# Two-stage packed attention and routed experts in one kernel: gate roots on VectorE, and new orders in the head, the first softmax and the last stores

## The chip, the cores and the metric

One core of a Trainium2 chip runs the whole kernel. The metric is the device time of one execution in microseconds (us), as the median of several runs; lower is better.

## The reference

```python
def sm_attn(qq, kk, vv):                       # per batch and head, head_dim 64
    s = scale * qq @ kk.T                      # scale = 1/8
    a = softmax(s)                             # row maximum taken off, sum + 1e-9
    return a @ vv
p_packed = sm_attn(p, k, v)                    # 32 packed rows of 576 keys
x = sm_attn(q, p_packed, p_packed)             # 576 queries on the 32 packed rows
# x: 8 batches of 576 tokens of 8 heads * 64 = 512 values
logits = unit(x) @ unit(expert_emb).T / tau    # 8 experts
e = argmax(logits); gate = softmax(logits)[e]
out = gate * (relu(x @ w1[e]) @ w2[e])         # 512 -> 1024 -> 512, all float32
```

With the inputs that are drawn, a batch's tokens nearly always go to one expert. The kernel guesses that expert for each batch and does the batch with it; tokens that went elsewhere would be done by a loop at the end.

## The kernel before

The order of the instructions is the order in which the Python code emits them; each engine runs its own instructions strictly in that order, and waits at the first whose operands are not ready. So an instruction that waits holds everything behind it on its engine.

Batch 0 is done by a function of its own, `begin`, and by `ffn(late=True)`. `begin` loads k, v and q of batch 0 whole, scores 32 packed queries against the keys, exponentiates (`key_exp`), turns the probabilities on TensorE (`p1_turn`), copies them out of PSUM (`p1_evac`), and multiplies by v (`pack_values`). Beside it runs the generator `embeddings`: it loads the expert embeddings, makes their norms by a Newton root on GpSimd (POOL), takes a reciprocal on VectorE (DVE, line 144), scales the embeddings on GpSimd (L147, `en_sb`), turns them on TensorE (L151) and copies them to `enT`. `itau` is 1/tau: tau comes by a DMA from ScalarE's (ACT's) queue, and line 1072 takes the reciprocal. `key_sum` makes the inverse sums `ri`. `guess` multiplies the summed packed rows by `enT` (L531), takes the maximum on VectorE and hands the expert's number to SyncE (SP) or GpSimd, whose queue then loads that expert's w1 and w2. After the guess, `begin` turns the queries q in four banks of four blocks and one of the two last blocks (L1093), copies them out by ScalarE and VectorE, and makes the query scores (L1153).

The second softmax of batch 0 (`att2(first=True)`) follows a table of steps, `ORDS`: U unpacks a half from PSUM (L576), B is the maximum, S takes it off, X is the exponential, T the sum and reciprocal (L596 to L598), N the multiplication, R the turn (L611), H the high part of the split into two float32r parts (L617), L the low part (L622). 0 and 1 are the two halves of the queries, a and b the two groups of heads. `ENG` says for S0, S1, N0, N1, L0, L1 and then for the four low parts of G (`split_g`, L267) whether GpSimd (p) or VectorE (v) does them.

`ffn` forms the hidden rows: `rows_w1` multiplies the packed rows by w1 in two parts (L838) and copies the products g32 to SBUF (L850, the second of each part on VectorE); `hidden` multiplies by the softmax (L870), first for the half 0 in float32, then for the half 1 from the split parts G and AT; ScalarE and VectorE write the two parts of hT (L874, L875). The 64 rows left over go by L905. Then come four blocks of 128 rows times w2 (L923, three passes over eight parts each, 24 matmuls for a block). Every block has a PSUM bank of 3 (`ps`, tag pf), and a bank comes free when `store` has multiplied it by the gate (L1223, ScalarE): the third block of L923 takes the bank of the 64 rows.

`route` multiplies AT by the packed rows (L674), five blocks in two banks (`pb`); VectorE reduces the logits (L683) and ScalarE the squares (L690), and only then is the bank free. `counts` (L716, L719) counts the tokens of each expert. `gates` makes the gate: a Newton root of the squares, the scaled logits (L737), an exponential on ScalarE (L741), its sum and a reciprocal (L744 to L749). The root is done by VectorE for batches 1 to 7 and by GpSimd for batch 0:

```python
for n, _ in enumerate(rsqrt(ss, y, "g", nc.gpsimd if x is bat[0] else nc.vector)):
```

While batch 0 goes through `ffn`, a table `PLAN` says for each step of it which other work is emitted: q is a step of `begin`, s of the softmax of batch 0, G a low part of G, a a step of the attention of batch 1, d a query flip of batch 1, w a part of w2, r a step of `route`, g a step of `gates`. From batch 1 on the loop at the end of the program hands the steps out by rule. The results leave by four DMAs of 32 rows for each block from SyncE's queue (L1236); the last block of the last batch is done and stored in two halves of 256 columns.

## Time and profile before

| what | value |
|---|---|
| median of 3 runs | 454.12 us (453.8 to 454.4) |
| the profiled execution | 454.63 us, its span in the trace 453.0 us |
| TensorE (PE) | busy 435.5 us, 96% |
| VectorE (DVE) | busy 295.8 us, 65% |
| ScalarE (ACT) | busy 204.2 us, 45% |
| GpSimd (POOL) | busy 152.2 us, 34% |

The page cuts the span into 40 slices of 11.3 us. TensorE is at 9 tenths or more in nearly all of them; the two slices from 68 to 91 us are the only ones before the last with a granted clock of 8 tenths rather than 9 or more. Times below are us from the span's start. Busy time of TensorE is modelled; a matmul that waits behind a running one can be counted as busy.

### The profile page before, as it was taken

Reading aid. Unit: us, or ns where it says so; the run is one execution under the profiler, and the core shown is the slowest. Engines: PE = TensorE matmul, PEld = TensorE weight load, DVE = VectorE, ACT = ScalarE, POOL = GpSimd, SP = SyncE. Lnnn points to the kernel's source line nnn. Section 1 sums busy time; section 2 is a strip of 40 time slices with the busy share of each in tenths; the row PEclk is TensorE's granted clock in tenths of the full one; section 3 lists DMA queues with packets and bytes.
Section 4 is the critical chain, followed back from the end, with each engine's and each line's share of the span. In section 5 each row is a group of like instructions: output and inputs, shape, how many; then the busy total and the mean of one; then the engine's idle time right before and its main releaser. Section 6 shows DMA issues by size and latency. Waiting matters only on the chain.

```text
span 453.0 us, 10735 instructions
## 1 busy us (share of the span) xinstructions
PE 435.5 (96%) x3908; PEld 343.3 (76%) x3909; DVE 295.8 (65%) x901; ACT 204.2 (45%) x479; POOL 152.2 (34%) x199
## 2 busy tenths in 40 slices
PE   8998995999999999999999999999999999999993
PEld 3758763869687987879687887879788886879783
DVE  5677638458994698648894688747895588635500
ACT  3557512375336551376335561376335651466210
POOL 2455682242703153042612244041621336033200
PEclk9999998899999999999999999999999999999997
DMA  8898597558698577866698576866597524710022
GB/s 235 300 264 235 153 267 252 149 134 226 182 342 231 148 200 256 262 164 178 171 372 225 155 200 221 280 181 177 157 376 211 140 52 167 264 26 23 14 49 52
DMA packets 39868, 87.12 MB, mean 192 GB/s; under 512 B 11768, under 2 KB 19192, under 8 KB 39808
## 3 DMA queue, kind: packets, MB, share of 16 engines
q1 hardware_dynamic: 31248, 56.52, 45.4%
q0 software_dynamic: 7840, 29.36, 18.0%
q8 instruction: 33, 0.54, 0.5%
q10 hardware_dynamic: 720, 0.48, 0.4%
q14 instruction: 27, 0.22, 0.2%
HBM read 76.89 MB, written 9.44 MB: 191 GB/s over the span
## 4 chain that ended last, share of the span: by engine, by line
PE 87%; DVE 4%; POOL 2%; ACT 2%; DMA 2%; issue 2%; SPq 0%; ACTq 0%; POOLq 0%; DVEq 0%
PE pf L923 38%; PE pf L870 23%; PE pf L905 6%; PE pt L674 6%; PE pt L252 3%; PE pt L803 3%; PE pt L373 2%; PE pt L356 2%; DMA emb_sb<-in_moe_expert_emb 1%; DMA nat<-in_k 0%; DVE mx L581 0%; PE pf L1093 0%; PE pf L838 0%; POOL w2r L768 0%; DVE st L576 0%
## 5 line engine op out<-in xcount | busy, mean ns | idle before, releaser
L923 PE MATMUL pf<-w2s,hT 128*128 128x512 f32 (+1 forms) x792 | 191.5, 394 | 5.4 <-ACT o L1223 5.4
L923 PEld LDWEIGHTS pf<-w2s,hT 128*128 128x128 f32 x792 | 144.2, 191 | 44.5 <-issue 8.9
L779 POOL TENSOR_TENSOR w2s<-w2r,w2s 128x512 fp32r<-128x512 f32 x64 | 82.4, 1289 | 220.6 <-ACT w2s L778 218.2
L870 PE MATMUL pf<-AT,G 128*128 128x288 f32 x720 | 105.7, 299 | 1.4 <-ACT T L1194 1.1
L870 PEld LDWEIGHTS pf<-AT,G 128*128 128x128 f32 x720 | 97.7, 188 | 7.0 <-issue 2.8
L875 DVE SCALAR_TENSOR_TENSOR hT<-pf,hT 128x224 fp32r<-128x224 f32 (+1 forms) x128 | 52.6, 415 | 32.7 <-ACT hT L874 32.6
L874 ACT ACTIVATE hT<-pf 128x224 fp32r<-128x224 f32 (+1 forms) x128 | 48.5, 384 | 48.5 <-PE pf L870 47.0
L690 ACT ACTIVATE at<-pt 128x512 f32<-128x512 f32 (+1 forms) x40 | 23.9, 597 | 38.9 <-DVE lg L683 38.0
L778 ACT CAST w2s<-w2r 128x512 fp32r<-128x512 f32 x64 | 39.2, 615 | 1.2 <-issue 1.2
L1223 ACT ACTIVATE o<-pf,gate 128x512 f32<-128x512 f32 (+1 forms) x41 | 25.9, 634 | 24.8 <-PE pf L923 17.8
L674 PEld LDWEIGHTS pt<-ppx,AT 128*128 128x128 f32 (+1 forms) x240 | 33.1, 177 | 4.6 <-ACT at L690 0.8
L674 PE MATMUL pt<-ppx,AT 128*128 128x264 f32 (+1 forms) x240 | 36.0, 286 | 0.3 <-ACT at L690 0.3
L905 PE MATMUL pf<-w2r,h 128*64 128x256 f32 x256 | 34.6, 391 | 0.0
L683 DVE TENSOR_REDUCE lg<-pt 128x8 f32<-128x16 f32 (+1 forms) x40 | 6.6, 164 | 35.4 <-PE pt L674 35.4
L817 DVE TENSOR_TENSOR G<-pt,G 128x512 fp32r<-128x512 f32 x28 | 18.8, 690 | 15.3 <-ACT G L816 15.3
L590 ACT ACTIVATE st<-st 128x576 f32<-128x576 f32 (+1 forms) x17 | 11.2, 660 | 36.3 <-DVE st L587 33.7
L905 PEld LDWEIGHTS pf<-w2r,h 128*64 128x64 f32 x256 | 15.5, 136 | 10.2 <-issue 4.7
L280 DVE STREAM_TRANSPOSE kt<-nat 128x576 f32<-128x576 f32 x28 | 21.4, 766 | 0.0
L741 ACT ACTIVATE lg<-lg 128x40 f32<-128x40 f32 x8 | 1.9, 236 | 42.7 <-DVE lg L737 42.7
L768 POOL DMA_DIRECT2D w2r<-in_moe_w x28 | 19.9, 714 | 0.4 <-issue 0.4
L617 ACT CAST AT<-at 128x576 fp32r<-128x576 f32 x16 | 10.8, 674 | 20.2 <-DVE at L611 20.2
L275 DVE STREAM_TRANSPOSE kt<-nat 128x576 f32<-128x576 f32 x28 | 19.2, 737 | 0.0
(186 smaller groups left out, 479.2 us busy)
## 6 DMA issues: line engine op xcount, KB each, us to landing
nat<-in_q SPq DMA_DIRECT2D x112, 140.0 KB, 3.1
w1t<-in_moe_w POOLq DMA_DIRECT2D x14, 1024.0 KB, 7.9
w2r<-in_moe_w POOLq DMA_DIRECT2D x28, 512.0 KB, 10.1
nat<-in_k SPq DMA_DIRECT2D x96, 140.0 KB, 3.2
vn<-in_v SPq DMA_DIRECT2D x46, 192.0 KB, 4.2
out<-o SPq DMA_DIRECT2D x124, 64.0 KB, 1.7
nat<-in_k SPq DMA_DIRECT2D x4, 576.0 KB, 5.2
w1t<-in_moe_w SPq DMA_DIRECT2D x4, 512.0 KB, 5.2
```

The lines of the kernel that those rows point to most:

```text
L280: nc.vector.transpose(kt.rearrange("p (c i) -> p c i", i=32), t)
L674: nc.tensor.matmul(pt[:r, 512 * g : 512 * g + XW], AT[:, a, g, c * P : c * P + r], x.ppx[:, m, g], start=(i == 0), stop=(i == 2),)
L690: nc.scalar.activation(scr[:r, :, : HB * D], ptv[:r, :, 0 : HB * D], AF.Square, accum_out=ss[:r, c : c + 1])
L768: queue.dma_start(t, w2e[:, 2 * i : 2 * i + 2, :])
L778: nc.scalar.copy(t[:, 0], raw)
L779: nc.gpsimd.tensor_tensor(out=t[:, 1], in0=raw, in1=t[:, 0].bitcast(F32), op=ALU.subtract)
L870: nc.tensor.matmul(pf[:, :HS], w, r, start=(n == 0), stop=(n == len(ops) - 1))
L874: nc.scalar.activation(hT[:, 0, f, cs], pf[:, :n], AF.Relu)
L875: nc.vector.scalar_tensor_tensor(out=hT[:, 1, f, cs], in0=pf[:, :n], scalar=0.0, in1=hT[:, 0, f, cs].bitcast(F32), op0=ALU.max, op1=ALU.su ...
L905: nc.tensor.matmul(pf[64 * hf : 64 * hf + 64, :256], h4[:, f], x.w2r[f // 2][:, f % 2, hf * 256 : hf * 256 + 256], start=(f == 0), stop=(f ...
L923: nc.tensor.matmul(pf[:, :w], hT[:, a, f, c * P : (c + 1) * P], x.w2s[f][:, m, at : at + w], start=(f == 0 and i == 0), stop=(f == NF - 1 ...
L1223: nc.scalar.activation(o[:, :w], pf[:, :w], AF.Copy, scale=x.gate[:, c : c + 1])
```

## The change

- The root of batch 0's gate goes to VectorE, as in the other batches.
- Head: the reciprocal of tau and the two copies of `p1_evac` come ahead of the reciprocal of the embeddings' norms; the two inverse sums become one pair of instructions on 128x2; six turns of q and their two copies come ahead of the guess, and three of the four large copies are ScalarE's (before: two).
- `ORDS`: R0b now ahead of B1. `ENG`: L1 on VectorE, the third low part of G on GpSimd. `PLAN`: other steps.
- The second half of the last stores: rows 64 to 127 from ScalarE's queue.

```diff
     def key_exp(x, g):
-        x.sums[g] = sm.tile([P, 1], F32, name="sums", tag="sums")
+        if g not in x.sums:
+            x.sums[g] = sm.tile([P, 1], F32, name="sums", tag="sums")
...
-        for n, _ in enumerate(rsqrt(ss, y, "g", nc.gpsimd if x is bat[0] else nc.vector)):
+        for n, _ in enumerate(rsqrt(ss, y, "g")):
...
+        sums, rinv = (
+            sm.tile([P, NG], F32, name=name, tag=name, bufs=1) for name in ("sums2", "rinv2")
+        )
+        for g in range(NG):
+            x.sums[g], x.rinv[g] = sums[:, g : g + 1], rinv[:, g : g + 1]
...
         next(emb_gen)
+        nc.vector.reciprocal(itau, itau)
+        p1_evac(x, 0, pt, 0)
         next(emb_gen)
-        p1_evac(x, 0, pt, 0)
-        nc.vector.reciprocal(itau, itau)
-        key_sum(x, 0)
         next(emb_gen)
-        key_sum(x, 1)
+        nc.vector.tensor_scalar(
+            out=rinv, in0=sums, scalar1=1e-9, scalar2=None, op0=ALU.add
+        )
+        nc.vector.reciprocal(rinv, rinv)
...
+        def queries(g, n, copy):
+            pu = bank()
+            turn(qn[g], pu, range(4 * n, 4 * n + 4))
+            copy(qT[:, g, 512 * n : 512 * n + 512], pu)
...
         both_rows(1)
+        pu = bank()
+        for g in range(NG):
+            turn(qn[g], pu[:, g * P :], (8,))
+        nc.scalar.copy(qT[:, :, 1024:], pu[:, : NG * P].rearrange("p (g s) -> p g s", g=NG))
+        queries(0, 0, nc.scalar.copy)
         g_guess = guess(x, 0, mybir.EngineType.SP, total)
...
         load_w1(x, x.e, 2)
-        pu = bank()
-        for g in range(NG):
-            turn(qn[g], pu[:, g * P :], (8,))
-        nc.scalar.copy(qT[:, :, 1024:], pu[:, : NG * P].rearrange("p (g s) -> p g s", g=NG))
-        for g in range(NG):
-            for n, copy in enumerate((nc.scalar.copy, nc.vector.tensor_copy)):
-                pu = bank()
-                turn(qn[g], pu, range(4 * n, 4 * n + 4))
-                copy(qT[:, g, 512 * n : 512 * n + 512], pu)
+        queries(0, 1, nc.scalar.copy)
+        queries(1, 0, nc.vector.tensor_copy)
+        queries(1, 1, nc.scalar.copy)
...
-                nc.sync.dma_start(
+                queue = nc.scalar if at and a >= 2 else nc.sync
+                queue.dma_start(
...
-        "U0a B0a S0a X0a U0b B0b S0b U1a T0a N0a X0b U1b T0b R0a N0b B1 R0b S1 X1 T1 N1 R1"
+        "U0a B0a S0a X0a U0b B0b S0b U1a T0a N0a X0b U1b T0b R0a N0b R0b B1 S1 X1 T1 N1 R1"
-    ENG = "ppppppppvp"
+    ENG = "pppppvpppp"
-        "aw", "awr", "adwr", "adr", "adwr", "adwr", "aw", "ar", "ag", "agr",
+        "aw", "awr", "adwr", "adr", "adwr", "adwr", "aw", "ar", "aag", "aagr",
...
```

The order on the engines, at three places. The first is VectorE in the head, between the two maxima of the first scores and the copy of the second turn; `enrm` belongs to the embeddings, `p1T` to the packed attention. Before:

```order
L336 TENSOR_REDUCE mx<-pt 128x1 x2
L144 RECIPROCAL enrm<-enrm 8x1
L365 COPY p1T<-pt 96x512
L366 COPY p1T<-pt 96x256
L1072 RECIPROCAL itau<-itau 128x1
L348 TENSOR_SCALAR ri<-sums 128x1
```

Now:

```order
L336 TENSOR_REDUCE mx<-pt 128x1 x2
L1076 RECIPROCAL itau<-itau 128x1
L366 COPY p1T<-pt 96x512
L367 COPY p1T<-pt 96x256
L144 RECIPROCAL enrm<-enrm 8x1
L1080 TENSOR_SCALAR rinv_210<-sums_209 128x2
```

The reciprocal of tau went ahead of both copies, that of the norms behind them.

The second place is VectorE at the end of batch 0's second softmax (`at_601` and `at_609` are the turned half 1, `g_557` to `g_598` and `g_549` to `g_589` the two parts of g32). Before:

```order
L581 TENSOR_REDUCE mx_522<-st 128x18
L611 STREAM_TRANSPOSE at<-st 128x288
L850 COPY g_557<-pf 128x512
L596 TENSOR_REDUCE s_564<-st 128x18
L597 TENSOR_SCALAR s_564<-s_564 128x18
L598 RECIPROCAL s_564<-s_564 128x18
L875 SCALAR_TENSOR_TENSOR hT<-pf,hT 128x288 x3
L850 COPY g_598<-pf 128x512
L611 STREAM_TRANSPOSE at_601<-st 128x576
```

Now:

```order
L851 COPY g_549<-pf 128x512
L612 STREAM_TRANSPOSE at<-st 128x288
L582 TENSOR_REDUCE mx_553<-st 128x18
L876 SCALAR_TENSOR_TENSOR hT<-pf,hT 128x288 x3
L851 COPY g_589<-pf 128x512
L597 TENSOR_REDUCE s_592<-st 128x18
L598 TENSOR_SCALAR s_592<-s_592 128x18
L599 RECIPROCAL s_592<-s_592 128x18
L876 SCALAR_TENSOR_TENSOR hT<-pf,hT 128x288 x2
L612 STREAM_TRANSPOSE at_609<-st 128x576
L876 SCALAR_TENSOR_TENSOR hT<-pf,hT 128x288 x2
L623 TENSOR_TENSOR AT<-at_609,AT 128x2x288
```

The first copy of g32 and the turn R0b went ahead of the maximum B1; the sum T1 went behind the second copy of g32; the low part L1 is new on VectorE.

The third place is the end of batch 0's routing. On TensorE the guess of batch 1 (`m`) stood ahead of the last route block (`64x264`). Before:

```order
L416 MATMUL pu<-enT,T 64x8 x4
L674 MATMUL pt<-ppx,AT 128x264 x6
L905 MATMUL pf<-w2r,h_527 64x256 x2
L536 MATMUL pu<-m_918,itau 1x8 x2
L674 MATMUL pt<-ppx,AT 64x264 x6
L905 MATMUL pf<-w2r,h_527 64x256 x2
L252 MATMUL pt<-kt,T 32x288 x16
```

Now:

```order
L417 MATMUL pu<-enT,T 64x8 x4
L675 MATMUL pt<-ppx,AT 64x264 x6
L906 MATMUL pf<-w2r,h_520 64x256 x2
L537 MATMUL pu<-m_931,itau 1x8 x2
L906 MATMUL pf<-w2r,h_520 64x256 x2
L252 MATMUL pt<-kt,T 32x288 x16
```

The guess is now behind the last route block, while VectorE still takes the guess's maximum ahead of that block's logits. On VectorE the root of batch 0's gate now stands there too, with an unpacking step of batch 1 (`st<-pt`) between its parts:

```order
L104 TENSOR_TENSOR rq_t<-rq_h,gy 128x5
L722 TENSOR_REDUCE cnt<-pu 1x8
L577 STREAM_TRANSPOSE st<-pt 128x288 x2
L106 TENSOR_TENSOR rq_t<-rq_t,gy 128x5
L109 SCALAR_TENSOR_TENSOR gy<-rq_t,gy 128x5
L734 TENSOR_TENSOR gy<-gy,ss 128x5
L735 TENSOR_SCALAR gy<-gy 128x5
L737 RECIPROCAL gy<-gy 128x5
L738 TENSOR_TENSOR lg<-lg,gy 128x40
```

Before, these root steps were GpSimd's, spread between four DMA issues and the splits of ppx, and the unpacking stood behind L737.

## Rows read from the trace of the kernel before

**Rows 1.** What TensorE waited for: line, releaser, us, times, longest.

```profile
PE pf L923 <- ACT o L1223: 5.4, 1, 5.4
PE pf L870 <- ACT T L1194: 1.1, 1, 1.1
```

**Rows 2.** Timeline of TensorE, 61 to 85 us: start, length, work, idle before.

```profile
61.62 10.07 PE L923 MATMUL pf<-w2s,hT 128*128 128x512 f32 x42
77.05 7.92 PE L923 MATMUL pf<-w2s,hT 128*128 128x512 f32 x21 [5.36 <-ACT o L1223]
```

**Rows 3.** Windows, 78 to 80 us: busy by engine, granted clock, DMA.

```profile
78.00:80.00 2.00, 2.00 (x6) 1.55 (x5) 1.42 (x4) 0.44 (x1) 0.98 (x1) 0.50 0.23 53
```

**Rows 4.** Timeline of ScalarE, the store.

```profile
76.54 0.46 ACT L1223 ACTIVATE o<-pf,gate 128x256 f32<-128x256 f32 x1
```

**Rows 5.** Timeline of VectorE, 58 to 86 us: root, gate, key flips.

```profile
58.36 2.29 DVE L93 TENSOR_SCALAR rq_i<-ss 128x5 int32<-128x5 int32 x1
...
68.77 0.17 DVE L733 TENSOR_TENSOR gy<-gy,ss 128x5 f32<-128x5 f32 x1 [6.86 <-POOL gy L114]
...
69.40 0.20 DVE L737 TENSOR_TENSOR lg<-lg,gy 128x40 f32<-128x40 f32 x1
69.52 0.84 DVE L576 STREAM_TRANSPOSE st<-pt 128x288 f32<-128x288 f32 x2
...
81.69 2.71 DVE L275 STREAM_TRANSPOSE kt<-nat 128x576 f32<-128x576 f32 x4
```

**Rows 6.** Timeline of GpSimd: DMA issues inside batch 0's root.

```profile
61.50 2.93 POOL L768 DMA_DIRECT2D w2r<-in_moe_w  x4 [0.38 <-issue]
```

**Rows 7.** Timeline of VectorE, 116 to 121 us: batch 1's root.

```profile
116.86 1.12 DVE L104 TENSOR_TENSOR rq_t<-rq_h,rq_i 128x5 f32<-128x5 f32 x1
...
120.45 0.17 DVE L734 TENSOR_SCALAR gy<-gy 128x5 f32<-128x5 f32 x1
```

**Rows 8.** Timeline of GpSimd, 116 to 122 us.

```profile
116.68 1.28 POOL L779 TENSOR_TENSOR w2s<-w2r,w2s 128x512 fp32r<-128x512 f32 x1
...
120.25 1.57 POOL L760 DMA_DIRECT2D w1t<-in_moe_w  x2 [2.10 <-DVE gy L109]
```

**Rows 9.** Timeline of VectorE, 55 to 57 us: guess, last logits.

```profile
55.23 0.14 DVE L540 MAX8 m<-pu 1x8 f32<-1x8 f32 x1
...
56.39 0.17 DVE L683 TENSOR_REDUCE lg<-pt 64x8 f32<-64x16 f32 x1 [0.32 <-PE pt L674]
```

**Rows 10.** Timeline of TensorE: query scores of batches 1 and 2.

```profile
56.87 1.94 PE L252 MATMUL pt<-kt,T 64*32 64x288 f32 x32
...
118.63 1.20 PE L252 MATMUL pt<-kt,T 64*32 64x288 f32 x32
```

**Rows 11.** Timeline of VectorE, head.

```profile
12.07 0.66 DVE L365 COPY p1T<-pt 96x512 f32<-96x512 f32 x1
```

**Rows 12.** The tile itau: its DMA (count, ns, first and last start) and landing.

```profile
L1024 ACTq DMA_DIRECT2D itau<-in_moe_tau x1: 359/359/359, 7.1 to 7.1; - x1
...
DMA to landing us min/median/max: 5.3/5.3/5.3
```

**Rows 13.** Timeline of GpSimd, head: scaling the embeddings.

```profile
12.24 1.59 POOL L147 TENSOR_SCALAR en_sb<-emb_sb,enrm 8x512 f32<-8x512 f32 x1 [0.28 <-DVE enrm L144]
```

**Rows 14.** Timeline of TensorE: turn of the embeddings.

```profile
14.37 0.41 PE L151 MATMUL pf<-ident,en_sb 8*128 8x8 f32 x4
```

**Rows 15.** Timeline of VectorE, 27 to 33 us.

```profile
27.60 0.76 DVE L596 TENSOR_REDUCE s<-st 128x18 f32<-128x576 f32 x1 [1.09 <-ACT st L590]
...
31.29 0.69 DVE L850 COPY g<-pf 128x512 f32<-128x512 f32 x1 [1.09 <-PE pf L838]
```

**Rows 16.** Timeline of GpSimd, 28 to 34 us.

```profile
29.00 1.16 POOL L602 TENSOR_TENSOR st<-st,s 128x576 f32<-128x576 f32 x1 [2.16 <-DVE s L598]
```

**Rows 17.** Timeline of TensorE: first hidden block of half 1.

```profile
35.90 1.18 PE L870 MATMUL pf<-AT,G 128*128 128x288 f32 x6
```

**Rows 18.** Timeline of SyncE's queue, the last stores.

```profile
446.40 1.76 SPq L1236 DMA_DIRECT2D out<-o  x4
```

4 lines of the change are left out of this document (2 added, 2 removed).

## The prediction

> **What bounds the kernel now.** I read the list of TensorE's waits first. It is short, and one entry stands out: 5.4 us before L923, ended by the store on ScalarE; what else stands there is a fifth of it or less, as the 1.1 us before L870 [rows 1]. TensorE is the bound everywhere else, so a change pays where TensorE waits or runs slowly. Then the timeline of TensorE there: 42 matmuls of L923 take 10.07 us, 0.24 each; TensorE stops at 71.69, goes on at 77.05, and the next 21 take 7.92 us [rows 2]. At 0.24 these would take 5.0, so 2.9 us more are lost. The window says why: the granted clock is 0.50, which is the 1.2 GHz level, where the stretches ahead run at 1.00 [rows 3]. Before the clock fell, TensorE had been idle since 71.69. The wait and the slow matmuls behind it are 5.4 + 2.9 = 8.3 us.
>
> Third, who holds the store back. It starts at 76.54 on ScalarE [rows 4], in whose order it stands behind both exponentials of batch 1; these need the unpacked scores from VectorE, which did nothing for 6.86 us, until GpSimd had finished the root of batch 0's gate; the root's last product is the scaled logits at 69.40 [rows 5]. The root is late because GpSimd issues four DMAs of 2.93 us in the middle of it [rows 6].
>
> **The change, part by part.** Times are on the clock of the trace of before; a shift of the head moves both sides of a wait alike and is left out until the sum.
>
> *Guess behind the last route block.* VectorE's guess, from 55.23 to 0.32 before 56.39, is 0.84 us [rows 9]; it now needs a product that TensorE makes only after the last route block and two L905. So the last logits end near 58.0 instead of 56.56. The scores L252 need the bank that these logits and the squares behind them free: the wait is already in the 1.94 us of batch 0's L252, which takes 1.20 in the next batch [rows 10]. TensorE has one more pair of L905 and the guess itself to do meanwhile (0.8), and the wait of 0.3 for the route bank is gone, so of 1.4 us about +0.7 stays (0 to 1.0).
>
> *Root on VectorE.* From the end of the last logits (56.56) to the root's start (58.36) took 1.8 us before [rows 5, 9], and I keep that: near 59.8. The root's nine small operations there pass at 0.2 each, about 1.8: 61.6. Then VectorE waits for the counts from TensorE, which came just ahead of the L923 of 61.62 [rows 2] and come 0.7 later, and reduces them (near 62.5); then the unpacking of 0.84 [rows 5] and the six last operations follow: the scaled logits at 64.6 instead of 69.40. From these to the store were 76.54 - 69.40 = 7.1 us [rows 4, 5], 0.8 of them the unpacking that is now done: 6.3, so the store starts near 70.9 and ends near 71.4. TensorE comes to the bank at 71.69 + 0.7 = 72.4. So the 5.4 goes, but with little to spare.
>
> What can take the spare is a collision. In batch 1, where VectorE already does the root, its first product took 1.12 us and ended with GpSimd's w2 split that had begun at 116.68 [rows 7, 8]. The Trainium skill, "SBUF — State Buffer", section "Who interferes with whom", has a rule against this change: a VectorE instruction with two SBUF inputs and a GpSimd instruction that reads SBUF exclude each other, and the second waits for the first to end. The 1.12 agrees with it. In the order of now GpSimd has all w2 splits behind it before its DMA issues begin, and the next to meet the root are two splits of ppx; one such wait costs up to the 0.95 of batch 1 (1.12 - 0.17). The store then ends at 72.3. I put 0.2 us of wait where 5.4 was: -5.2. Without the long idle time the clock should stay at 1.00: -2.9.
>
> *After it.* TensorE now reaches batch 1's route matmuls 8 us sooner, and their banks need logits that VectorE makes behind four key flips of 2.71 us [rows 5]. Before, the flips were done in time; now the third route block meets them nearly. I take +0.4 (0 to 0.9).
>
> *Head.* The reciprocal of tau is now ahead of both copies. Tau lands 5.3 us after its issue at 7.1, near 12.4 [rows 12]; the first copy began at 12.07 [rows 11]. So VectorE waits for tau, the copies start at 12.6 (+0.5), and the reciprocal of the norms comes behind them, near 13.5 instead of 11.99. GpSimd then scales the embeddings for 1.59 us [rows 13], to 15.3, and TensorE's turn of them, which started at 14.37 [rows 14], can't start before 15.4: +1.0. This cover was 0.5 us before and is gone. The six turns of q ahead of the guess then fill TensorE's short wait for `total` ahead of the guess and leave less behind it; I take half of the 1.0 or a little more to come back so, and the query scores to come +0.4 later (0 to 1.0). w1's DMA is issued a us later too, since the guess is; its second part was just in time, so the first hidden block pays another 0.2 (0 to 0.7), with R0b ahead of B1 giving back what it can.
>
> *First softmax, half 1.* T1 ran at 27.60; now it stands behind the second copy of g32, which waits for TensorE until 31.29 and ends at 31.98 [rows 15]. T1 with its two small followers is 1.2 (to 33.2), N1 on GpSimd 1.16 [rows 16] (34.4), and the turn, the high part and the low part, all of 128x576 as the sum is, are taken at its 0.76 each (36.7); with one hT between, and a GpSimd split beside the low part, it is near 37.3. TensorE wants it at about 35.9 [rows 17]. So a wait of 1.4 us opens there, and another of about 0.8 behind it, since hT of that block follows the maximum and exponential of batch 1 as before; the old 1.1 us wait [rows 1] for the same exponential merges into these: +1.1 net. The bounds are wide: -1.1, if only the old wait goes and nothing replaces it, to +1.6.
>
> *Last stores.* The four last issues took 1.76 us on one queue, 0.44 each [rows 18]. Two of them go out beside the other two: the last starts 0.8 us sooner, and nothing follows but its landing: -0.8 (0 to -1.9, if its landing is shortened as well).
>
> The joined inverse sums replace four short instructions with two on an engine that waits there anyway: 0.
>
> **The sum**: -5.2 - 2.9 + 0.7 + 0.4 + 0.4 + 0.2 + 1.1 - 0.8 = -6.1 us. The profiled execution took 454.63 (span 453.0) and the median is 454.12; the same step taken from each gives 448.5 and 448.0. I forecast **448.0 us**.
>
> **The rivals.**
> 1. *The head gains, as its new order reads.* R0b comes earlier by the maximum that stood ahead of it, T1 doesn't hold up the half 1, and the old 1.1 us wait goes. For it: only the wait for tau is a row; the rest of the head's price is worked out through several engines. Against it: engines run in order, and the second copy of g32 can't be earlier than its matmuls. The head's +1.7 becomes about -1.3: 445.0.
> 2. *The root is still late, because VectorE waits for GpSimd's DMA issues.* `rq_i` took 2.29 us at 58.36, through the end of such an issue [rows 5]; now it meets a train of six issues (1.57 and 2.93 [rows 6, 8]) and would end near 64: the store ends 3 us late, and part of the clock's loss returns: 451 to 454, say 452.5. The same page of the Trainium skill gives a reason for it: the lock is shared with descriptor writing for some VectorE operations. Against it: in batch 1 a small operation at 120.45 took 0.17 under the issue at 120.25 [rows 7, 8], and the other six batches repeat this.
> 3. *Slower: the root's products are held, one after another.* Seven products of the root, each held 0.95 us as the one at 116.86 was [rows 7], are 6.7 us; the wait for the bank returns with about 6, the clock falls again, and the head's +1.7 and the guess's +0.7 remain: 457. It decides from about four held products on, where the bank's wait is 3 us and the clock falls as well. Against it: only one of seven was held in each later batch, and GpSimd has few operations to hold with at that place.
> 4. *The change doesn't reach the wait*, because the store still stands behind both exponentials on ScalarE, and these are not earlier: 5.4 and 2.9 stay, about +1 from the rest: 455 less what the tail gives, 454.5. Against it: the first unpacking is ahead of the root's end in the new order, so the exponentials move with it.
>
> **How the numbers follow.** A measurement of this kernel tells about 0.2%, 0.9 us, from no change. The forecast, from 446.5 to 450.5, has 0.52; the head's gain 0.25 (444 to 446.5); the late root 0.14 (450.5 to 454); no reach 0.04; slower 0.05. Faster takes the first two and most of the third: 0.90; within 0.2% 0.05; slower 0.05. The range of 8 in 10 goes from 444.5, which takes in most of the head's gain, to 451.5, which takes in a third of the late root's.
>
> **What would show it.** In the new profile: no wait of TensorE for the store, or one under 1 us; granted clock 1.00 from 70 to 90 us; the scaled logits some 4.8 us earlier against the first L923 of batch 0. In the head: VectorE's reciprocal of tau not before 12.4, the turn of the embeddings near 15.4, the query scores 0.4 later than before. At the first block of half 1, a wait of 1 to 1.5 us, and L252 longer than 1.94. The last store issues from two queues. I am wrong if the root's small operations last longer than 0.2 us each, if the clock falls in spite of TensorE's being busy, or if the half 1 starts without a wait.

## The result and the profile after

The changed kernel takes 447.91 us in the median of four runs (446.96 to 448.25); the kernel before took 453.96 in the same comparison (453.06 to 454.4). The ratio is 0.9866, its 95% interval 0.9844 to 0.9888: faster, and by far more than 0.2%. The forecast was 448.0 in a range of 444.5 to 451.5.

The profiled execution of the changed kernel took 446.96 us, its span 445.3. That is the fastest of the four, while the profiled execution of before (454.63) is above its median, so the two traces differ by 7.7 us and the medians by 6.1. I come back to this.

TensorE's waits in the changed kernel (line, releaser, us, times, longest), which answer to [rows 1]:

```profile
PE pf L839 <- DMA w1t<-in_moe_w: 1.3, 1, 1.3
...
PE pf L871 <- DVE AT L623: 1.2, 1, 1.2
PE pt L675 <- ACT at L691: 0.9, 1, 0.9
PE pf L871 <- DVE h L881: 0.8, 1, 0.8
PE pt L252 <- ACT at L691: 0.6, 1, 0.6
```

The 5.4 us before the third block of w2 products are 0.3 now, and the 1.1 us for T are gone. The five lines shown are short waits, none over 1.3; of them only the one for the route bank was in the list before, with 0.3. The longest, for the DMA of w1, lies in the head and comes up again at the end. The timeline of TensorE there (start, length, work, idle before), against [rows 2]:

```profile
61.65 10.04 PE L924 MATMUL pf<-w2s,hT 128*128 128x512 f32 x42
72.02 4.45 PE L924 MATMUL pf<-w2s,hT 128*128 128x512 f32 x18 [0.34 <-ACT o L1235]
...
80.28 1.74 PE L675 MATMUL pt<-ppx,AT 128*128 128x264 f32 x12 [0.95 <-ACT at L691]
...
84.08 1.95 PE L804 MATMUL pt<-w1t,T 64*32 64x512 f32 x32
```

and the window from 78 to 80 us (busy time of the engines, then the granted clock), against [rows 3]:

```profile
78.00:80.00 2.00, 1.33 (x9) 0.85 (x7) 1.52 (x5) 0.46 (x1) 0.64 (x3) 1.00 0.47 115
```

TensorE stops at 71.68 for 0.34 us and goes on at the rate of before the wait: 18 matmuls in 4.45 us, 0.25 each. The clock is 1.00, the 2.4 GHz level, where it was 0.50. What is new is the 0.95 us at 80.28, the wait for a bank of batch 1's route.

The timeline of VectorE at the root, against [rows 5]:

```profile
59.56 0.17 DVE L93 TENSOR_SCALAR rq_i<-ss 128x5 int32<-128x5 int32 x1
...
62.78 0.66 DVE L109 SCALAR_TENSOR_TENSOR gy<-rq_t,gy 128x5 f32<-128x5 f32 x1
63.48 0.67 DVE L734 TENSOR_TENSOR gy<-gy,ss 128x5 f32<-128x5 f32 x1
64.18 0.66 DVE L735 TENSOR_SCALAR gy<-gy 128x5 f32<-128x5 f32 x1
...
65.10 0.20 DVE L738 TENSOR_TENSOR lg<-lg,gy 128x40 f32<-128x40 f32 x1
```

and that of GpSimd, against [rows 6]:

```profile
58.77 1.75 POOL L761 DMA_DIRECT2D w1t<-in_moe_w  x2 [0.33 <-DMA nat<-in_k]
60.51 2.83 POOL L769 DMA_DIRECT2D w2r<-in_moe_w  x4
63.36 1.44 POOL L267 TENSOR_TENSOR ppx<-pp,ppx 128x256 fp32r<-128x256 f32 x2
```

The first instruction of the root, `rq_i`, passes in 0.17 us under GpSimd's w1 issue. Three of the last ones are held to 0.66 or 0.67 where 0.17 is usual, beside the end of the w2 issues and the two splits of ppx. The scaled logits stand at 65.10. Counted from the first w2 block of batch 0 (59.78 now, 59.75 before) they are 4.3 us earlier; 4.8 was forecast. The store on ScalarE's timeline, which answers to [rows 4], is

```profile
71.51 0.46 ACT L1235 ACTIVATE o<-pf,gate 128x256 f32<-128x256 f32 x1
```

which is 0.6 behind the forecast 70.9: the three held instructions cost 3 x 0.49 = 1.5, and a part of it is made up, since the counts, for which VectorE waits in the middle of the root, were reduced by 61.9 and not near 62.5. TensorE came to the bank at 71.68 and not at 72.4, so the 1.0 us to spare that the forecast had became a wait of 0.34.

### The profile page after: what moved, and what is told of

It is laid out like the page before. It is cut to its first block, busy times and chain, and to the rows that moved or that the text cites. A ratio compares the mean times of both kernels' runs of the same rounds, so it can differ in the third digit from the quotient of the medians.

```text
span 445.3 us, 10738 instructions
## 1 busy us (share of the span) xinstructions
PE 431.5 (97%) x3908; PEld 341.0 (77%) x3909; DVE 297.6 (67%) x908; ACT 205.2 (46%) x480; POOL 149.3 (34%) x186
## 4 chain that ended last, share of the span: by engine, by line
PE 88%; DVE 5%; DMA 3%; ACT 2%; issue 1%; SPq 0%; POOL 0%; ACTq 0%; POOLq 0%
PE pf L924 37%; PE pf L871 22%; PE pf L906 7%; PE pt L675 7%; PE pt L252 3%; PE pt L804 3%; PE pt L374 2%; PE pt L357 2%; DMA w1t<-in_moe_w 1%; DMA pn<-in_p 1%; DMA out<-o 1%; PE pt L230 1%; DVE kt L275 1%; ACT p L342 1%; DVE mx L336 0%
## 5 line engine op out<-in xcount | busy, mean ns | idle before, releaser
L924 PE MATMUL pf<-w2s,hT 128*128 128x512 f32 (+1 forms) x792 | 188.8, 390 | 0.3 <-ACT o L1235 0.3
L924 PEld LDWEIGHTS pf<-w2s,hT 128*128 128x128 f32 x792 | 142.3, 188 | 38.3 <-issue 8.9
L591 ACT ACTIVATE st<-st 128x576 f32<-128x576 f32 (+1 forms) x17 | 11.2, 659 | 33.1 <-DVE st L588 33.1
```

What stands on the lines that cost most here:

```text
L924: nc.tensor.matmul(pf[:, :w], hT[:, a, f, c * P : (c + 1) * P], x.w2s[f][:, m, at : at + w], start=(f == 0 and i == 0), stop=(f == NF - 1 ...
```

## Where the time went, in five stretches

Of every profiled kernel I took the same six instants: the first score matmul of batch 0, the block of half 0 behind the second w1 part, the first product of the 64 rows, the first w2 block of batch 0, the end of ScalarE's last store, the end of the span. The differences, in us, worked out from the timelines of TensorE and ScalarE (each ratio is to the runs of before in the same comparison; the kernels below the second row are those of the next section):

```
                          head and  half 1 to  64 rows    w2 block to  last store  median  ratio to before
                          half 0    64 rows    and route  last store   to end      us      (95% interval)
before                    24.62     16.71      11.88      386.62       6.65
changed                   23.46     17.60      12.20      379.77       5.73        447.91  0.9866 (.9844-.9888)
changed again             23.93     17.58      12.21      379.62       5.72        447.85  0.9872 (.9847-.9897)
root alone                25.04     16.70      11.87      380.85       6.77        448.93  0.9895 (.9879-.9910)
root back                 24.24     17.57      12.19      384.26       6.11        452.82  0.9983 (.9970-.9996)
steps back                25.34     17.57      12.21      379.50       5.84        449.21  0.9902 (.9883-.9921)
one store queue           23.78     17.58      12.21      379.63       7.33        448.45  0.9882 (.9865-.9899)
head back                 24.12     17.60      12.21      379.72       5.95        447.83  0.9860 (.9839-.9881)
softmax back              23.71     16.63      11.87      382.02       6.03        448.38  0.9883 (.9861-.9905)
tau late                  23.33     17.59      12.21      379.65       5.87        447.65  0.9864 (.9837-.9890)
tau late, low part early  22.61     17.95      12.21      379.57       6.02        447.46  0.9863 (.9839-.9886)
tau late, split late      23.76     18.00      12.21      379.84       6.07        448.05  0.9881 (.9857-.9904)
route between flips       23.45     18.02      12.21      380.18       6.13        448.57  0.9893 (.9873-.9913)
tau late, old softmax     24.13     16.28      12.19      379.70       5.89        446.74  0.9844 (.9826-.9861)
```

The columns two to four repeat from profile to profile within 0.15 us where the code is the same, better than the times of whole runs, which spread over 0.7 to 2.7 us for one kernel. The first column doesn't repeat: with the head of the changed kernel it is 23.46, 23.71, 23.78, 23.93, 24.24 and 25.34. In root alone, root back and head back it holds a fall of TensorE's clock as well (see the head). So an edit is judged by the stretch that it touches, and by the ratios only where they differ by more than their intervals; each kernel has one profile, the changed kernel two.

## The experiments

**The root alone.** The kernel before with the root on VectorE and nothing else.

```diff
-        for n, _ in enumerate(rsqrt(ss, y, "g", nc.gpsimd if x is bat[0] else nc.vector)):
+        for n, _ in enumerate(rsqrt(ss, y, "g")):
```

> The kernel before with one edit: the root of batch 0's gate on VectorE. Theory (the root alone removes the wait): the scaled logits come near 64 us instead of 69.40, the store 7.1 us behind them, near 71; TensorE reaches the bank at 71.7 and waits under 1 us instead of 5.4; the clock stays up (2.5 us back, as the changed kernel shows: from the end of the wait to the first w1 product of batch 1 are 12.06 us with 0.95 of waiting in it, before 13.58); the route banks of batch 1 then make TensorE wait up to 0.95. Time 446.5 to 448, against 454.0 before. Rival (the batch 1 steps drawn ahead are needed too): the store still stands 3 us or more late, the clock falls, time 450 to 453.

448.93 us: this one line has 4.8 of the change's 6.1 us (1 - 0.9895 of 453.45). The wait is 1.16, not under 1, and the time is 0.9 above the range that the theory gave. The clock stays up. The timeline of VectorE in this kernel shows what remains:

```profile
59.49 2.29 DVE L93 TENSOR_SCALAR rq_i<-ss 128x5 int32<-128x5 int32 x1
```

beside it GpSimd's:

```profile
58.69 1.75 POOL L760 DMA_DIRECT2D w1t<-in_moe_w  x2 [0.32 <-issue]
60.46 1.29 POOL L779 TENSOR_TENSOR w2s<-w2r,w2s 128x512 fp32r<-128x512 f32 x1
```

and TensorE's:

```profile
73.98 5.15 PE L923 MATMUL pf<-w2s,hT 128*128 128x512 f32 x21 [1.16 <-ACT o L1223]
...
82.24 1.00 PE L674 MATMUL pt<-ppx,AT 128*128 128x264 f32 x6 [0.95 <-ACT at L690]
```

`rq_i` lasts 2.29 us again, to the length of [rows 5], and ends within 0.1 us of GpSimd's w2 split that stands between its two trains of issues. In the kernel before it is the same; there the split was

```profile
59.33 1.29 POOL L779 TENSOR_TENSOR w2s<-w2r,w2s 128x512 fp32r<-128x512 f32 x1
```

and `rq_i` ended at 60.65, 0.03 behind it. The changed order has that split ahead of both trains, and there `rq_i` takes 0.17 under the same issue. So the second rival of the prediction has the place right, but it read the wait of before as one to the end of an issue, and it ends with the split: in all three profiles where a split stood there (before, root alone, softmax back) `rq_i` took 2.29, in all eleven others 0.16 or 0.17. And the 0.95 us at the route bank is here too: it comes with the earlier arrival of TensorE, and needs no other part of the change.

**The root back.** The changed kernel with that line undone.

```diff
-        for n, _ in enumerate(rsqrt(ss, y, "g")):
+        for n, _ in enumerate(rsqrt(ss, y, "g", nc.gpsimd if x is bat[0] else nc.vector)):
```

> The changed kernel with one edit undone: the root of batch 0's gate on GpSimd again, all the rest as changed. Theory (the root is the cause): GpSimd again issues DMAs in the middle of the root, the scaled logits come at 68 to 70, the store 6.3 us behind them at 75 to 76; TensorE waits 3.5 to 5 us for it and the clock falls again for 2 to 3 us: 452.5 to 455. Rival (the steps of batch 1 that were drawn ahead free the store): a wait under 1.5 us, 448 to 449.5.

452.82 us. TensorE's timeline in this kernel:

```profile
77.79 5.87 PE L924 MATMUL pf<-w2s,hT 128*128 128x512 f32 x18 [4.77 <-ACT o L1235]
```

VectorE's, where it gets the root from GpSimd:

```profile
70.24 0.17 DVE L734 TENSOR_TENSOR gy<-gy,ss 128x5 f32<-128x5 f32 x1 [6.21 <-POOL gy L114]
```

and three windows of 2 us behind the wait (the granted clock is the third number from the end):

```profile
78.00:80.00 2.00, 2.00 (x5) 1.60 (x6) 1.93 (x5) 0.67 (x1) 0.23 (x1) 0.50 0.22 52
80.00:82.00 2.00, 2.00 (x8) 1.55 (x7) 0.96 (x3) 0.00 (x0) 1.24 (x1) 0.77 0.10 26
82.00:84.00 2.00, 2.00 (x13) 1.69 (x12) 1.97 (x6) 1.26 (x2) 1.16 (x1) 1.00 0.00 0
```

The theory holds: the wait is back at 4.77, the clock is 0.50 behind it, and all other parts of the change together are worth 0.2% without the root. The clock is up again in the window from 82; before, it was 0.50 until 82 and 0.71 from 82 to 84. The loss by the clock is therefore not one number: behind idle times of 4.77 and 5.36 us, it was 1.4 us here (18 matmuls in 5.87 against the changed kernel's 4.45) and 2.8 in the profiled execution of before (21 in 7.92 [rows 2] against the 5.15 of root alone).

**The steps of batch 1 back.**

```diff
-        "aw", "awr", "adwr", "adr", "adwr", "adwr", "aw", "ar", "aag", "aagr",
+        "aw", "awr", "adwr", "adr", "adwr", "adwr", "aw", "ar", "ag", "agr",
```

> The changed kernel with the two steps of batch 1 that stand ahead at the gate taken back (one step fewer in each of two places). In its order the store stands between the two exponentials of batch 1 on ScalarE, no longer behind both. Theory (what is left of the wait hangs on the exponentials ahead of the store): the store comes 1 to 2 us earlier, the wait of 0.34 goes, the wait of 0.95 for the route bank changes by less than 0.5 either way as batch 1 comes two steps later: 447 to 448.3, the same as the changed kernel within 0.2%. Rival (the steps ahead are needed): batch 1 comes late, its route or first hidden block waits 1 us or more: 449 to 450.

The store stands between the two exponentials and is early on ScalarE's timeline:

```profile
71.05 0.45 ACT L1235 ACTIVATE o<-pf,gate 128x256 f32<-128x256 f32 x1
```

TensorE's shows 66 matmuls without a stop:

```profile
64.32 15.60 PE L924 MATMUL pf<-w2s,hT 128*128 128x512 f32 x66
...
83.14 1.00 PE L675 MATMUL pt<-ppx,AT 128*128 128x264 f32 x6 [1.03 <-ACT at L691]
```

From the first w2 block (62.46) to the store are 8.6 us, in the changed kernel 11.7. The wait of 0.34 is gone, the one at the route bank is 1.03, and the stretch is 0.27 shorter than the changed kernel's (0.12 against its second profile). The median of 449.21 is 0.9 us above the expected range all the same and in that of the rival, whose wait of 1 us or more at the route is there too, if only 0.1 longer than in the changed kernel. The profile doesn't bear the rival out: its stretch isn't longer, and its excess is in its head, 25.34, which this edit doesn't touch. What the five other runs, 447.71 to 450.38, owe to it isn't shown. So the two steps ahead are not needed for the gain at the bank, and giving them back gains 0.1 to 0.3 us there.

**One queue for the last stores.**

```diff
-                queue = nc.scalar if at and a >= 2 else nc.sync
+                queue = nc.sync
```

> The changed kernel with the last four stores on SyncE's queue alone, as before. Theory: the end comes 0.8 to 0.9 us later (two issues of 0.44 us each behind the other two, and nothing else follows), the stretch from the end of ScalarE's last store to the end of the span 6.6 us instead of 5.75: 448.7. Rival (the landing hides it): no change, within 0.2 us.

The last stretch is 7.33 us, where the other kernels with two queues have 5.7 to 6.1, and the two with the old stores 6.65 and 6.77. The two queues are worth 0.9 (before against changed) to 1.6 us; 0.8 was forecast. Why one queue gives 7.33 here and 6.65 and 6.77 in the kernels with the old stores isn't shown. The ratios of whole runs can't tell this from nothing (0.9882 against 0.9866 and 0.9872).

**The head.** Four profiles of the changed head had shown by then that tau doesn't land at one time. VectorE's timeline has the reciprocal of tau in the changed kernel at

```profile
11.18 0.16 DVE L1076 RECIPROCAL itau<-itau 128x1 f32<-128x1 f32 x1 [0.20 <-DMA itau<-in_moe_tau]
```

with the root back at 12.37, with one store queue at 12.07 and with the steps back at

```profile
13.75 0.16 DVE L1076 RECIPROCAL itau<-itau 128x1 f32<-128x1 f32 x1 [1.50 <-DMA itau<-in_moe_tau]
```

The wait for it is 0.20, 1.25, 0.92 and 1.50 us in this order. So the first profile of the changed kernel, in which the step of the prediction on tau looks wrong, was the lucky one. The next comparison has a second look at the changed kernel, the changed kernel with the whole head as before (the head's part of the change turned round), and one, called tau late, with the reciprocal of tau behind the two copies and that of the norms ahead of them as before, and nothing else put back:

```diff
-        nc.vector.reciprocal(itau, itau)
-        p1_evac(x, 0, pt, 0)
         next(emb_gen)
+        p1_evac(x, 0, pt, 0)
+        nc.vector.reciprocal(itau, itau)
         next(emb_gen)
```

> The changed kernel itself once more, for this comparison. If the first profile of it was one with an early tau, its times spread over 2 us with a median of 447.5 to 449, and this profile shows VectorE's wait for tau of about 1 us and TensorE's wait of 0.5 us for the scaled embeddings. If the wait is rare, the median is near 447.5 and the wait is 0.2 us as in the first profile.

> The changed kernel with the whole head of batch 0 as before (reciprocal of tau behind the copies, that of the norms ahead of them, four short instructions for the inverse sums, all turns of q behind the guess). Theory (the new head costs): tau landed at 11.2 us in the first profile of the changed kernel, but at 12.1, 12.4 and 13.8 in three others with the same head, and there VectorE waited 0.9 to 1.5 us for it, and TensorE 0.5 us for the scaled embeddings; with the old head that wait goes, the guess stands 0.8 us or more earlier against the first score matmul, w1 lands as much earlier: 0.5 to 1.2 us faster than the changed kernel in the same comparison. Rival (the new head gains, since its six turns fill TensorE's wait ahead of the guess): 0.3 to 0.8 us slower.

> The changed kernel with one thing of its head undone: the reciprocal of tau behind the two copies and that of the norms ahead of them, as before; joined sums and turns of q ahead of the guess stay. Theory (the wait for tau is the head's price): VectorE no longer waits for tau, the copies start near 11.4 us or as soon as the turn is done, the turn of the embeddings right behind the product with v, without the 0.5 us wait; 0.6 to 1.2 us faster than the changed kernel in the same comparison, and a little faster than with the whole old head. Rival (tau is hidden by the later landing of q or w1): the same within 0.3 us.

The changed kernel came to 447.85 with a wait for tau of 0.58, between the two that were expected, the old head to 447.83, tau late to 447.65. By the medians the three are the same within 0.2 us, so they show neither the gains of the two theories nor the 0.3 to 0.8 of loss of the old head's rival, and agree with the rival of tau late; the intervals are too wide to rule out half a us. The stretches say more: from the first score matmul to VectorE's `total` are 8.2 us with the old head, 8.7 with tau late and 9.0 in the changed kernel. Over all fourteen profiles it is 8.2 to 8.8 in the eight in which the reciprocal of tau stands late, and 8.7 to 10.3 in the six in which it stands early, so tau does cost there when it lands late. The head and half 0 take 24.12, 23.33 and 23.93. But TensorE's clock falls in the head of some kernels and not of others, and that is as large as what was looked for: the first 18 turns of q take 3.8 us in root alone and head back, and 2.2 in the kernel before. Two windows with the old head (PE's busy time is the second number, the granted clock the third from the end):

```profile
14.00:16.00 2.00, 1.59 (x55) 1.43 (x44) 0.87 (x4) 0.82 (x3) 1.15 (x2) 1.00 0.96 336
16.00:18.00 2.00, 2.00 (x18) 1.96 (x14) 0.75 (x5) 0.87 (x3) 0.90 (x2) 0.60 0.63 244
```

and the same with tau late:

```profile
14.00:16.00 2.00, 2.00 (x53) 1.76 (x41) 0.82 (x3) 1.11 (x4) 1.18 (x2) 1.00 1.05 402
16.00:18.00 2.00, 2.00 (x25) 1.75 (x23) 1.09 (x6) 1.63 (x4) 0.87 (x2) 1.00 0.51 197
```

TensorE was busy for 1.59 us of the two from 14 to 16 in the first, and 2.00 in the second. A clock of 0.52 to 0.63 in the windows from 16 to 20 us stands in three of the fourteen profiles (root alone, root back, head back), two of them with the old head. These busy times alone don't tell which execution falls: from 14 to 16 TensorE was busy for 1.59 us in the kernel before too, for 1.48 with the steps back and 1.49 with one store queue, and the clock stayed at 1.00 in all three. With so few profiles, and none of the old head and new softmax without such a fall, what the new order of the head gives or costs in time is open within about 0.5 us; that TensorE works where it used to wait ahead of the guess may be worth a fall of the clock now and then, which I only argue and no run shows.

**The first softmax.**

```diff
-        "U0a B0a S0a X0a U0b B0b S0b U1a T0a N0a X0b U1b T0b R0a N0b R0b B1 S1 X1 T1 N1 R1"
+        "U0a B0a S0a X0a U0b B0b S0b U1a T0a N0a X0b U1b T0b R0a N0b B1 R0b S1 X1 T1 N1 R1"
...
-    ENG = "pppppvpppp"
+    ENG = "ppppppppvp"
...
-        "qsssqsssssssqsqssss", "qq", "sss", "", "G", "s", "G", "", "s", "sG",
-        "sG", "s", "sa", "aq", "a", "aqs", "aq", "aws", "aqs", "awq",
+        "qsssqsssssssqsqssssss", "qqs", "s", "s", "sG", "", "G", "", "s", "s",
+        "sG", "a", "aG", "aq", "a", "aqs", "aq", "aws", "aqs", "awq",
```

> The changed kernel with the order of the first softmax, its split engines and the first steps of the plan as before (R0b behind B1, low part of half 1 on GpSimd, third low part of G on VectorE, T1 ahead of the second copy of g32). From the traces so far the new order takes 4.2 to 4.6 us from the first hidden block to the block behind the second w1 part, where the old took 5.5 to 5.7, and 17.6 from there to the 64 rows, where the old took 16.7. Theory (a gain of 1.1 to 1.5 in the first half, a loss of 0.9 in the second, both due to this part): the two stretches return to 5.5 to 5.7 and 16.7, the time is 0.2 to 0.6 us longer than the changed kernel's. Rival (the head's order caused one of the two): a stretch stays as in the changed kernel, the time moves by 0.9 or more either way.

Half 1 takes 16.63 again: the new order costs 0.95 us there, as forecast. The other half of the theory fails: from the first hidden block to the block behind the second w1 part are 4.29 us and not 5.5 to 5.7, as the rival had it (4.19 in the changed kernel). With the old head and the old softmax this piece takes 5.69 (before) and 5.52 (root alone), with the old head and the new softmax 4.61 (head back), so in these profiles either of the two new orders gets most of it. Root alone and head back are alike up to that first hidden block (19.52 and 19.51 us from the first score matmul), so with the old head the new softmax gains 0.9 there and loses 0.9 in half 1. With the new head it gains 0.1 there, with tau late 0.3 (4.61, and 4.95 in the last kernel below). The sum is 0.5 us slower than the changed kernel, for a reason that neither theory had: the old plan draws one step of batch 1 ahead, and with that the order at the root shifts. VectorE's timeline:

```profile
57.67 2.29 DVE L93 TENSOR_SCALAR rq_i<-ss 128x5 int32<-128x5 int32 x1
```

ScalarE's:

```profile
72.10 0.67 ACT L618 CAST AT<-at 128x576 fp32r<-128x576 f32 x1 [1.14 <-DVE at L612]
72.68 0.47 ACT L1235 ACTIVATE o<-pf,gate 128x256 f32<-128x256 f32 x1
```

and TensorE's:

```profile
73.19 6.00 PE L924 MATMUL pf<-w2s,hT 128*128 128x512 f32 x18 [2.24 <-ACT o L1235]
```

A w2 split stands between the issues again and holds `rq_i` for 2.29 us, and the store has gone behind one more instruction of batch 1 on ScalarE, the cast of AT. The wait is 2.24 and the clock falls. The last kernel below differs from this one in that step and in tau, and there `rq_i` takes 0.17 and the wait is 0.32. So one more step of batch 1 ahead costs 2.3 us in the stretch behind the first w2 block, and the two steps fewer of above gain 0.1 to 0.3: the stall was not removed with room to spare.

**Two repairs of half 1 that don't work.** The wait of 1.17 us at half 1 ends with its low part on VectorE. VectorE's timeline in the changed kernel:

```profile
35.14 0.46 DVE L876 SCALAR_TENSOR_TENSOR hT<-pf,hT 128x288 fp32r<-128x288 f32 x1 [0.71 <-ACT hT L875]
35.51 0.85 DVE L623 TENSOR_TENSOR AT<-at,AT 128x576 fp32r<-128x576 f32 x1
```

and GpSimd's, with the two late splits of G:

```profile
33.23 2.51 POOL L267 TENSOR_TENSOR G<-g,G 128x512 fp32r<-128x512 f32 x2
```

The first repair is tau late with the low part one step earlier:

```diff
-        "sG", "s", "sa", "aq", "a", "aqs", "aq", "aws", "aqs", "awq",
+        "sG", "ss", "a", "aq", "a", "aqs", "aq", "aws", "aqs", "awq",
```

> As the run with the reciprocal of tau late, and the low part of half 1 one step earlier, so that VectorE takes it ahead of one part of hT, not behind it. Theory (the wait of 1.17 us at the first block of half 1 ends with that low part, which stood behind the hT of 35.14): it starts about 0.7 us earlier and the wait shrinks to 0.3 to 0.6 us; 0.5 to 0.8 us faster than with tau late alone, about 446.5. Rival (hT moves behind it and the bank of hT is late next): the wait of 0.76 at a later block grows by as much, no change.

VectorE's timeline in it:

```profile
33.87 1.53 DVE L623 TENSOR_TENSOR AT<-at,AT 128x576 fp32r<-128x576 f32 x1 [0.40 <-ACT AT L618]
```

and GpSimd's:

```profile
32.28 2.51 POOL L267 TENSOR_TENSOR G<-g,G 128x512 fp32r<-128x512 f32 x2
```

The low part starts ahead of the hT, as meant, and then lasts 1.53 us instead of 0.85; in both kernels it ends 0.6 us behind the end of GpSimd's two splits of G (34.79 and 35.74). The wait at half 1 is 1.16 as before. The Trainium skill, "SBUF — State Buffer", section "Who interferes with whom", has it that a VectorE instruction with two SBUF inputs contends with a GpSimd instruction that reads SBUF, for ports that it calls an exclusive lock. The low part is such a one, and these rows agree. Neither the theory (a wait of 0.3 to 0.6) nor the rival (a growing 0.76) came true. The next kernel is tau late with one of the two splits taken away from there:

```diff
-        "sG", "s", "sa", "aq", "a", "aqs", "aq", "aws", "aqs", "awq",
+        "s", "s", "sa", "aqG", "a", "aqs", "aq", "aws", "aqs", "awq",
```

> As the run with the reciprocal of tau late, and the fourth low part of G three steps later, behind the low part of half 1. Where the low part of half 1 was begun 0.7 us earlier it lasted 1.53 us instead of 0.85 and ended 0.6 us behind the end of GpSimd's two G splits, as in the changed kernel. Theory (VectorE's product with two SBUF inputs waits for GpSimd's splits): with one split instead of two in front, it ends 0.9 to 1.3 us earlier and lasts 0.7 to 0.9; TensorE's wait of 1.17 us at half 1 falls to 0.4 or less; 0.5 to 1.0 us faster than with tau late alone, if the later wait of 0.76 doesn't grow. Rival (the low part waits for its high part on ScalarE, not for GpSimd): the wait stays over 0.9 us.

VectorE's timeline:

```profile
35.40 0.46 DVE L876 SCALAR_TENSOR_TENSOR hT<-pf,hT 128x288 fp32r<-128x288 f32 x1 [0.70 <-ACT hT L875]
35.77 0.75 DVE L623 TENSOR_TENSOR AT<-at,AT 128x576 fp32r<-128x576 f32 x1
```

and GpSimd's:

```profile
33.50 1.28 POOL L267 TENSOR_TENSOR G<-g,G 128x512 fp32r<-128x512 f32 x1
```

The split ends at 34.78, a microsecond ahead of the low part, which still starts at 35.77, behind the hT, and takes its 0.75. The wait is 1.07, over the rival's 0.9, and the stretch is 0.4 longer with the late split. Both covers hold the low part to the same time: without the splits it stands behind the hT, without the hT behind the splits. Taking both away was not tried.

**The route between the key flips.** The kernel before this one (tau and the split late), and:

```diff
-        second = att2(x, keys_main(b + 1) if b else None, b == 0, b < 1, ENG1 if b == 1 else "vvvvvv")
+        second = att2(x, keys_main(b + 1) if b > 1 else None, b == 0, b < 1, ENG1 if b == 1 else "vvvvvv")
...
-        if b:
+        if b == 1:
+            yield from alternate(keys_main(b + 1), route(x))
+        elif b:
             yield from route(x)
```

> As the run with tau and the split late, and batch 1's five route blocks emitted between the key flips of batch 2, not behind all four. Theory (the 0.95 us wait for a route bank comes from 2.7 us of flips in front of the logits): the logits of the first block come before the third flip, the wait of 0.95 falls below 0.3, 0.5 to 0.9 us faster than without this edit, 445.8 to 446.8. Rival (the route matmuls come earlier than the low part of batch 1's probabilities, which GpSimd ends near 78.5, and wait for that): a wait of 0.7 us or more at the route, no gain.

TensorE's timeline:

```profile
76.51 0.90 PE L675 MATMUL pt<-ppx,AT 128*128 128x264 f32 x6
...
80.87 1.00 PE L675 MATMUL pt<-ppx,AT 128*128 128x264 f32 x6 [1.34 <-ACT at L691]
```

and ScalarE's, the square of the first block:

```profile
80.13 0.60 ACT L691 ACTIVATE at<-pt 128x512 f32<-128x512 f32 x1 [0.94 <-POOL AT L623]
```

The logits of the first block do come behind one flip, and the wait grows to 1.34. TensorE comes to the route 1.4 us earlier than in the changed kernel, counted from the first w2 block, while the square that frees the bank is only 1.0 earlier: it now waits for GpSimd's low part of AT, whose input has the same tag (`at`) as the square's scratch tile. The rival had the right engine; the flips were one cover of two here as well.

**Tau late and the old softmax, without the step ahead.** The last kernel puts together what the stretches spoke for: tau late, the lines of `ORDS` and `ENG` and the first steps of the plan as in softmax back, and one step less in the plan. Of its diff, the plan:

```diff
-        "qsssqsssssssqsqssss", "qq", "sss", "", "G", "s", "G", "", "s", "sG",
-        "sG", "s", "sa", "aq", "a", "aqs", "aq", "aws", "aqs", "awq",
+        "qsssqsssssssqsqssssss", "qqs", "s", "s", "sG", "", "G", "", "s", "s",
+        "sG", "", "aG", "aq", "a", "aqs", "aq", "aws", "aqs", "awq",
```

> The changed kernel with the reciprocal of tau late and the order of the first softmax and its split engines as before, but without the one step of batch 1 that the old plan drew ahead there, so that TensorE's order is the changed kernel's, and the store of the 64 rows stands where it stands there. Theory (half 1 loses 0.95 us by the new softmax order, and the head about 0.5 to 0.8 by tau): from the block behind the second w1 part to the 64 rows 16.6 to 16.8 us instead of 17.6, the stretch before it 4.2 to 4.6, the wait at the bank of the 64 rows 0.3 to 0.5, no fall of the clock; time 446.0 to 447.2, 0.9 us or more under the changed kernel. Rival (without the step the maxima and exponentials of batch 1 come later and make half 1 wait in another place): 17.3 us or more for that stretch, 447.5 to 448.5.

TensorE's timeline:

```profile
31.01 5.12 PE L871 MATMUL pf<-at,g 128*128 128x288 f32 x20
35.75 1.17 PE L871 MATMUL pf<-AT,G 128*128 128x288 f32 x6
...
47.29 0.65 PE L906 MATMUL pf<-w2r,h 128*64 128x256 f32 x4
...
71.71 4.45 PE L924 MATMUL pf<-w2s,hT 128*128 128x512 f32 x18 [0.32 <-ACT o L1235]
```

446.74 us (446.5 to 447.2), 0.9844 of before (0.9826 to 0.9861). Half 1 to the 64 rows takes 16.28 us, below the 16.6 to 16.8 of the theory, without the 1.17 us wait of the changed kernel and without the 1.1 of before [rows 1]; the piece ahead of it takes 4.95, longer than the 4.2 to 4.6 of the theory; the bank's wait is 0.32. It is the fastest kernel of this study. Against the changed kernel, 447.91 and 447.85, that is 1.1 us or 0.25%; the intervals of the ratios overlap, but its slowest of five runs is below the median of either series of the changed kernel.

## Why the prediction came out right, and where not

**The bank's wait and the root.** Forecast 5.4 to 0.2, measured 5.36 to 0.34. Undone and done alone, the root is the cause. Rival 4, that the change doesn't reach the wait, falls with the root alone. Rival 3, that the root's products are held one after another, came true for three instructions, at 0.49 us each; that is below the four that the prediction named as the point of decision. Instructions of more than 0.2 us were also one of its signs of being wrong: the sign came, and the forecast held, since 1.5 us of holding left a wait of 0.34 only.

**The clock.** Forecast -2.9. In the kernel before, the first w1 product of batch 1 was

```profile
90.63 2.20 PE L803 MATMUL pt<-w1t,T 64*32 64x512 f32 x32
```

From the end of the wait to it were 13.58 us before and are 12.06 now, 0.95 of them a wait: -2.5. The loss with the root back was about half of that of before. The mechanism is right; the size differed between these two profiles.

**The route banks.** Forecast +0.4 (0 to 0.9), measured +0.95: the step took the third block to meet the flips "nearly", and it meets them in full. It is the term of this stretch that was most mis-sized.

**The guess behind the route.** Forecast +0.7, measured 12.20 - 11.88 = +0.3, with the wait inside L252 (0.64). The sum of the step doesn't come out: 1.4 less the 0.8 of other work and less the 0.3 for the route bank is 0.3, not 0.7. And the last logits came only 0.95 later and not 1.4 (they end 9.64 us behind the first product of the 64 rows, 8.69 before).

**Half 1.** Forecast +1.1 net, with waits of 1.4 and 0.8; measured waits 1.17 and 0.76, net +0.9, and +0.95 when undone.

**The head.** Forecast +0.4 for tau and +0.2 for w1. The wait for tau is real, 0.20 to 1.50 us in six profiles, but its landing was taken from one profile as if it were a fixed time. The signs that hung on it did not come in the first profile: the reciprocal at 11.18 (not before 12.4), the turn of the embeddings at 14.19 (near 15.4). Counted from the first score matmul, the query scores came 0.6 and 0.2 us earlier in the two profiles of the changed kernel (11.21 and 11.59, before 11.82), not 0.4 later. The term for w1 was too small: TensorE waits 1.3 us for its DMA, the longest wait of the changed kernel, where 0.2 (0 to 0.7) was forecast. Together the first hidden block comes at 19.26 and 19.74 instead of 18.93, +0.3 and +0.8, so that this sum is about right through two errors.

The step that failed is the next one, half 0, in which I let R0b only "give back what it can" and put nothing: from the first hidden block on it took 4.20 and 4.19 instead of 5.69. A part of this may be the wait for w1, which now stands ahead of the piece. Head and half 0 together take 23.46 and 23.93 where before took 24.62: -1.2 and -0.7 for a forecast of +0.6. This is the largest miss, 1.3 to 1.8 us in the two profiles of the changed kernel, and the gain that the first rival had claimed for the head is in part there, beside the loss in half 1 that it had denied. Other kernels with the same head had 23.7 to 25.3, so the size is not a fixed one.

**The last stores.** Forecast -0.8, measured -0.9, and 1.6 when undone.

**The sum.** The traces differ by -7.7 where the terms gave -6.1: -1.8 from the head, +0.9 from the clock and the route, -0.4 from the guess, the rest small. That the median is right to 0.1 us owes something to chance: terms that were off by 0.4 to 1.8 us cancel in part. The step was taken from medians, and the two traces are not median executions: the one of before is at 454.63 with a median of 453.96, the one of the changed kernel is 0.95 below its median, with the earliest tau of all. In the kernel before the mean granted clock goes from 0.986 to 0.993 from run to run, and the profiled run has 0.987, so part of its clock's loss isn't in every run.

## What to carry to other kernels

When an engine that waits is freed, ask of each instruction behind the old wait what its second cover is: the low part of half 1 stood behind an hT and behind two splits, the route bank behind flips and behind another engine's low part, and removing one cover gained nothing. Judge small edits by the stretch of the trace that they touch, taken between instants that repeat, and by more than one profile where a DMA's landing is in the stretch. Where work is handed out by a table, look at what one step more or less does at the place that was just repaired; here one step more cost 2.3 us.

## What the runs showed of the hardware that I had not expected

A small VectorE instruction with one input of 128x5 was held to the end of a GpSimd split in three kernels (2.29 us each time), though it had started while GpSimd was still issuing DMAs, a microsecond ahead of the split; under the same issue with no split behind it, it took 0.16 or 0.17 in eleven. Under the second train, the w2 issues, other instructions of the root did take 0.60 to 0.70. The Trainium skill, "SBUF — State Buffer", section "Who interferes with whom", has instructions with at most one SBUF input free of such waits only outside its 2-port modes, and counts `tensor_scalar` among those that can enter them. `rq_i`, and the last TENSOR_SCALAR of the root with its 0.66, are of that kind and were held, so these rows don't speak against the page; no run shows in which mode they ran. Which of the two, the issue or the split behind it, takes hold of `rq_i` isn't settled.

The time at which a DMA of one value for each partition landed moved from 11.2 to 13.8 us after the span's start in profiles of the same head. And the clock fell without a long wait, too: in three of fourteen profiles it fell near 16 us, where no wait of TensorE between 7 and 16 us had been longer than 0.9.
